# Attention outputs kept as queries x columns, their sums from a ones column in V, spilled as rows and read back transposed

## The chip, the cores and the metric

The kernel runs on one core of one Trainium2 chip. The metric is the device time of one execution in microseconds (us). TensorE (PE, with its weight loads PEld) multiplies, VectorE (DVE) and ScalarE (ACT) read its results in PSUM, GpSimd (POOL) works on SBUF alone, and SyncE (SP) issues nearly all DMAs.

## The reference

Two independent layers on 2048 tokens of width 1024; their outputs stand side by side.

```python
# A: a diagonal state-space layer (complex), P = D = 1024
Bu = einsum('bld,pd->blp', x, B_bar)
h[t] = Lam_bar * h[t-1] + Bu[t]                       # for every token
a = 2 * einsum('blp,dp->bld', h, C).real + x * Dskip
# B: attention over 64 segments of 32 tokens, 32 heads of 128, 8 memory tokens
for s in range(64):
    h = concat([mem, x[32*s:32*s+32]])                # 40 tokens
    q, k, v = h @ Wq, h @ Wk, h @ Wv                  # per head
    p = softmax(mask(q @ k.T / sqrt(128)))
    o = (p @ v) @ Wo
    mem, out_s = o[:8], o[8:]
return concat([a, b], -1)                             # bf16
```

## The kernel before

**Phase one** (`p1`, 0 to about 363 us) works on eight blocks `pc` of 128 states and, in step, on eight blocks `hb` of four heads. `stage1` forms B x for one block and 512 tokens on PE, scans it on DVE and writes the states to DRAM (`a_hs`). `v_x` computes V for four heads and 128 tokens per step; ACT copies it into `b_vst`, a tile for four steps with two buffers, and SP writes it to DRAM (`b_vx`). `load_wv` brings Wv by blocks, two buffers. `og` multiplies per-segment means of the tokens with the Wv block.

**Phase two** (`p2`, about 364 to 497 us) runs `stage2`: 32 halves, each of 16 matmuls of 512 columns (L289) from the states (`a_hl`, read back per 512 tokens) and C; DVE adds x * Dskip, which POOL has formed. Between halves the main loop puts the last two `og` (blocks 0 and 1) and the eight steps of `guess`, which multiply `ogT` with Wo (`b_wog`, 2 MB pieces, two buffers) to guess the memory tokens of all segments. The guesses become further columns of `b_xe`; `v_mem` computes their V rows.

**Attention** (`p3`, about 500 to 1071 us) goes over 16 pairs of heads `hp`, 11 units `u` each. A unit has two groups of three segments: a group is 96 tokens and 3 memory rows, 99 in all (`GW`), so a unit holds four 99 x 99 blocks (two groups, two heads). `att_front` forms four score blocks with keys on partitions and queries along the columns, takes Exp on ACT and multiplies the mask on POOL (`b_m`). `att_back`, two units later, multiplies a matrix of ones with `b_m`, so that every partition has the column sums (`psR`), takes 1/sum as Exp(-Ln) on ACT, and multiplies V (as weights) with the block: the result has head columns on partitions and queries along the columns, which is the form that the output projection needs as weights. DVE multiplies it by 1/sum into `b_ot`; SP writes `b_ot` to DRAM (`b_os`) for the first 14 pairs, the last two pairs stay in SBUF. Memory rows go to `b_omT`. The generator `proj` feeds Q and K of later pairs: 18 steps a pair, of 8 matmuls of 480 columns (L492) or 16 of 201 (L477), spread over the units, ten steps ahead.

**Output projection** (`p4`, about 1071 to 1315 us): for four blocks of 512 tokens `load_o` brings the spilled outputs (`b_ol`); each group of 32 matmuls (one per head, L607) gives 128 tokens and half of the 1024 columns. `wo0` and `wo1` are the halves of Wo, the second loaded into the space of `b_xe` when the projections are done. `check` tests the guessed memory against the computed one and sets a flag; if the guess failed, a general loop would run. It doesn't run here.

The order on each engine is made by a planner: it takes instructions in the order of the program where they are ready by its own model of time, and may draw a later instruction ahead. `keep_in_program_order` ties an instruction to its place. Tiles have a fixed number of buffers, and an instruction that needs a buffer or reused space waits for its last reader.

Of the kernel before, what the change touches and what calls it, by code (L numbers as in the profile page):

```python
# [26 lines left out]
HB = 8; HP = 16  # L27
# [8 lines left out]
NM = NTL + NMX  # L36

# [84 lines left out]
class PartA:  # L122
# [137 lines left out]
    def stage2(self, pool):  # L260
# [12 lines left out]
        for tb in range(NB):  # L273
            hl = []
            for q in range(4):
                hl.append(pool.tile([128, 2, 2, TB], BF16, name=f"a_hl{q}", bufs=2))
                (q0 if tb == 0 else k.SP).dma_start(hl[q][:], self.hs[tb][:, 2 * q:2 * q + 2, :, :])
            for tt in range(4):
                t0 = tb * TB + tt * 128
                xn = xns.pop(4 * tb + tt)  # L280
                xd = pool.tile([128, D], FP32, name="a_xd", bufs=2)
                G.tensor_tensor(xd[:], xn[:], dB[:], ALU.mult)
                ot = pool.tile([128, D], BF16, name="a_ot", bufs=2)
                for half in range(2):
                    hs = slice(half * 512, (half + 1) * 512)
                    py = k.ps("O")
                    for pc in range(PC):
                        for i in range(2):
                            PE.matmul(py[:], hl[pc // 2][:, pc % 2, i, tt * 128:(tt + 1) * 128], self.CT[:, i, pc, hs],  # L289
                                      start=(pc == 0 and i == 0), stop=(pc == PC - 1 and i == 1))  # L290
                    V.tensor_tensor(ot[:, hs], py[:], xd[:, hs], ALU.add)
                    yield
                k.SP.dma_start(self.out[0, t0:t0 + 128, 0:D], ot[:])
                if 4 * tb + tt + 3 < TT:
                    load_xn(4 * tb + tt + 3, k.SP)

class PartB:
    def __init__(self, k, x, mem0, Wq, Wk, Wv, Wo, out):  # L300
# [4 lines left out]
        self.vx = [k.drp.tile([NSLOT, 512], BF16, name=f"b_vx{i}") for i in range(HB)]  # L305
        self.vt = [k.drp.tile([NTL, 512], BF16, name=f"b_vt{i}") for i in range(HB)]
        self.os = [k.drp.tile([128, 8, T], BF16, name=f"b_os{i}") for i in range(4)]
        c = k.cst
        self.m0T = c.tile([128, KC, M], BF16, name="b_m0T")
        self.omT = c.tile([128, H, NM], BF16, name="b_omT")  # L310
# [4 lines left out]
        self.accR = c.tile([128, HP * NU], FP32, name="b_accR")  # L315
# [3 lines left out]
    def init(self, tmp):  # L319
# [11 lines left out]
        z = tmp.tile([32, 512], BF16, name="b_zero", bufs=1)  # L331
        k.V.memset(z[:], 0.0)
        for hb in range(HB):
            k.G.dma_start(self.vx[hb][64 + NMX:GX, :], z[0:GX - 64 - NMX, :])
            k.G.dma_start(self.vx[hb][T + 32:NSLOT, :], z[0:32, :])

# [37 lines left out]
    def v_x(self, hb, w):  # L374
        k = self.k
        vx = self.vx[hb]
        for q in range(4):
            st = self.wl.tile([128, 4, 512], BF16, name="b_vst", bufs=2)
            for i in range(4):
# [4 lines left out]
                k.copy("s", st[:, i, :], p[:])  # L384
# [4 lines left out]
            k.SP.dma_start(vx[s0:s0 + n * 128, :].rearrange("(i p) n -> p i n", p=128), st[:, 0:n, :])  # L389
            if q == 3:  # L390
                k.SP.dma_start(vx[0:64, :], st[0:64, 3, :])
                k.SP.dma_start(vx[T - 32:T + 32, :], st[64:128, 3, :])
# [3 lines left out]
    def og(self, hb, w, tag="R"):  # L396
        k = self.k
        p = k.ps(tag)
        for h in range(4):
            for c in range(KC):  # L400
                k.PE.matmul(p[:, h * NSEG:(h + 1) * NSEG], w[:, c, h * 128:(h + 1) * 128], self.xbar[:, c, :], start=(c == 0), stop=(c == KC - 1))
        k.V.tensor_copy(self.ogT[:, hb * 4:(hb + 1) * 4, :], p[:, 0:4 * NSEG].rearrange("p (h s) -> p h s", h=4))


    def guess(self, pool):
        k = self.k; V, PE = k.V, k.PE
        pg = k.ps("S")
        for q in range(4):
            wo = pool.tile([128, H, 256], BF16, name="b_wog", bufs=2)
            k.SP.dma_start(wo[:], self.Wo[:, :, q * 256:(q + 1) * 256])  # L410
# [21 lines left out]
    def v_mem(self, hb, w=None):  # L432
# [5 lines left out]
        st = self.wl.tile([128, 4, 512], BF16, name="b_vst", bufs=2)  # L438
        k.copy("v", st[0:NM, 0, :], p[0:NM, :])
        k.SP.dma_start(self.vx[hb][64:64 + NMX, :], st[0:NMX, 0, :])  # L440
        k.SP.dma_start(self.vt[hb][:], st[NMX:NM, 0, :])
# [58 lines left out]
    def load_v(self, hp):  # L500
        if hp < HP:
            k = self.k
            vt = self.p3a.tile([GW, NG, 256], BF16, name="b_v", bufs=2)
            hb, cs = hp // 2, slice((hp % 2) * 256, (hp % 2) * 256 + 256)
# [4 lines left out]
    def att_front(self, hp, u):  # L509
        k = self.k; PE = k.PE  # L510
# [9 lines left out]
        m = self.p3a.tile([GW, 2, 2, GW], BF16, name="b_m", bufs=4)  # L520
        mask = k.maskA if u == 0 else k.maskB
        k.G.tensor_tensor(m[:], e[:], mask[0:GW, :, :].unsqueeze(2).to_broadcast([GW, 2, 2, GW]), ALU.mult)  # L522
        return m

    def att_back(self, hp, u, m):
        k = self.k; PE, V = k.PE, k.V
        vt = self.vtile[hp]
        sm = k.ps("R")
        W4 = 4 * GW
        mf = m[:].rearrange("p a b q -> p (a b q)")  # L530
        PE.matmul(sm[:, 0:W4], k.ones[0:GW, :], mf, start=True, stop=True)
        ln = self.p3a.tile([128, W4], FP32, name="b_ln", bufs=2)
        r = self.p3a.tile([128, 2, 2, GW], FP32, name="b_r", bufs=2)
        i = hp * NU + u
        k.S.activation(ln[:], sm[:, 0:W4], ACT.Ln)  # L535
        k.S.activation(r[:].rearrange("p a b q -> p (a b q)"), ln[:], ACT.Exp, scale=-1.0, accum_out=self.accR[:, i:i + 1])  # L536
        o = k.ps("O", (128, 2, 2, GW))
        for gg in range(2):
            for hh in range(2):
                PE.matmul(o[:, gg, hh, :], vt[:, 2 * u + gg, hh * 128:(hh + 1) * 128], m[:, gg, hh, :], start=True, stop=True)  # L540
        ot = self.ot[hp]
        V.tensor_tensor(ot[:, :, 2 * u * GX:(2 * u + 2) * GX].rearrange("p h (g n) -> p g h n", n=GX),  # L542
                        o[:, :, :, 0:GX], r[:, :, :, 0:GX], ALU.mult)
        om = self.omT[:, 2 * hp:2 * hp + 2, :]
        V.tensor_tensor(om[:, :, 6 * u:6 * u + 6].rearrange("p h (g n) -> p g h n", n=3),
                        o[:, :, :, GX:GW], r[:, :, :, GX:GW], ALU.mult)
        if u == 0:
            V.tensor_tensor(om[:, :, NTL:NM], o[:, 0, :, 64:64 + NMX], r[:, 0, :, 64:64 + NMX], ALU.mult)
            if hp >= HP - 2:
                k.G.tensor_copy(ot[:, :, NSLOT:NSLOT + 64], ot[:, :, 0:64])  # L550
                k.G.tensor_copy(ot[:, :, NSLOT + 64:NSLOT + 128], ot[:, :, GX:GX + 64])
        if u == NU - 1:
            del self.vtile[hp]
            if hp < HP - 2:
                os = self.os[hp // 4]; h0 = (hp % 4) * 2
                k.SP.dma_start(os[:, h0:h0 + 2, 0:64], ot[:, :, 0:64])
                k.SP.dma_start(os[:, h0:h0 + 2, 64:T], ot[:, :, GX:T + 32])

    def att_init(self):
        self.vtile, self.ot = {}, {}  # L560
        self.load_v(0)

    def attention(self):
        units = [(hp, u) for hp in range(HP) for u in range(NU)]
        pend = []
        for n, (hp, u) in enumerate(units):
            if u == 0:
                self.load_v(hp + 1)
                self.ot[hp] = self.p3a.tile([128, 2, NSLOT + 128], BF16, name="b_ot", bufs=2)
            pend.append((hp, u, self.att_front(hp, u)))  # L570
            if len(pend) > 2:
                self.att_back(*pend.pop(0))
            yield hp, u
        for p in pend:
            self.att_back(*p)
            yield HP, 0


    def load_o(self, tb):
        k = self.k  # L580
        t = self.p4.tile([128, 28, 512], BF16, name="b_ol", bufs=2)
        for q in range(4):
            n = 8 if q < 3 else 4
            k.SP.dma_start(t[:, 8 * q:8 * q + n, :], self.os[q][:, 0:n, tb * 512:(tb + 1) * 512])
        return t

    def outproj(self, tb, ol):
# [5 lines left out]
        for tt, half in order:  # L593
# [6 lines left out]
            for h in range(H):  # L600
                if h < 28:
                    lhs = ol[:, h, tt * 128:(tt + 1) * 128]
                else:
                    ot = self.ot[h // 2]
                    s0 = NSLOT if t == 0 else t * 128 + 32
                    lhs = ot[:, h % 2, s0:s0 + 128]
                PE.matmul(p[:], lhs, self.wo[half][:, h, :], start=(h == 0), stop=(h == H - 1))  # L607
# [6 lines left out]
    def check(self):  # L614
# [3 lines left out]
        def small(name, n):  # L618
            return pool.tile([128, n], FP32, name=name, bufs=1)
        dn = small("c_dn", 4)  # L620
        V.memset(dn[:], 0.0)
        for half in range(2):
            hs = slice(half * 512, (half + 1) * 512)
            p = k.ps("P")
            for h in range(H):
                PE.matmul(p[0:NM, :], self.omT[:, h, :], self.wo[half][:, h, :], start=(h == 0), stop=(h == H - 1))
# [13 lines left out]
        for i, acc in enumerate((self.accE, self.accR)):  # L640
            a = small("c_a", HP * NU)
# [113 lines left out]
def kernel_main(tc, A_x, A_Lre, A_Lim, A_Bre, A_Bim, A_Cre, A_Cim, A_logdt, A_Dskip, B_x, B_mem0, B_Wq, B_Wk, B_Wv, B_Wo, out,  # L755
                force=False, dbg=None):
    with ExitStack() as ctx:
# [73 lines left out]
        with pool("p2", "right") as p2:  # L831
            g = b.guess(p2)
            s2 = a.stage2(p2)
            wv = [wv, b.load_wv(1)]
            for i, _ in enumerate(s2):
                if i in (2, 4):
                    b.og(i // 2 - 1, wv[i // 2 - 1], "P")
                if i > 4 and i % 2 == 1:
                    next(g, None)
                if i == 16:  # L840
# [10 lines left out]
        with pool("p3b", "right") as p3b:  # L851
# [7 lines left out]
            for n, (hp, u) in enumerate(at):  # L859
# [5 lines left out]
                while done < want:  # L865
                    next(pr)
                    done += 1
        xs.close()
# [17 lines left out]
        p3.close()  # L886
# [68 lines left out]
```

## Time and profile before

| | |
|---|---|
| Median of 8 runs | 1315.62 us (1313.8 to 1320.58) |
| Profiled execution | 1317.0 us, span 1315.2 us, mean granted clock 0.989 |
| PE busy | 1273.8 us, 97% of the span |
| DVE, ACT, POOL busy | 674.0, 427.3, 211.1 us |
| DMA | 163.15 MB, mean 124 GB/s |

All positions are microseconds from the start of the span. A row of the timeline has the start, the time from the first start to the last end of what it merges, the engine, the line, the operation with the tiles it writes and reads, and in brackets how long the engine had been idle and what released it. A matmul's recorded duration holds its latency: 512 columns show some 380 ns, but in a stream they start 216 ns apart, so that starts give the price. A transfer's bytes move after its issue.

### The profile page before, as it was taken

Reading aid. Unit: us, or ns where it says so; the run is one execution under the profiler, and the core shown is the slowest. Engines: PE = TensorE matmul, PEld = TensorE weight load, DVE = VectorE, ACT = ScalarE, POOL = GpSimd, SP = SyncE. Lnnn points to the kernel's source line nnn. Section 1 sums busy time; section 2 is a strip of 40 time slices with the busy share of each in tenths; the row PEclk is TensorE's granted clock in tenths of the full one; section 3 lists DMA queues with packets and bytes.
Section 4 is the critical chain, followed back from the end, with each engine's and each line's share of the span. In section 5 each row is a group of like instructions: output and inputs, shape, how many; then the busy total and the mean of one; then the engine's idle time right before and its main releaser. Section 6 shows DMA issues by size and latency. Waiting matters only on the chain. (4 is left out here: it accounts for less than half of the span.)

```text
span 1315.2 us, 20149 instructions
## 1 busy us (share of the span) xinstructions
PE 1273.8 (97%) x7874; PEld 659.7 (50%) x7874; DVE 674.0 (51%) x1500; ACT 427.3 (32%) x1135; POOL 211.1 (16%) x291
## 2 busy tenths in 40 slices
PE   6899899999969999999999999999999999999997
PEld 2344444444435545555555555555555544444443
DVE  6999999988821224555555555555555530001000
ACT  3333333333310001554555444545554440001000
POOL 5000000000112220222222222222222220000000
PEclk9999999999979999999999999999999989999999
DMA  9993433444389519324343434323332470403000
GB/s 229 258 212 110 120 107 108 123 129 138 115 261 309 187 48 250 83 86 121 99 133 99 133 99 133 99 85 96 87 84 83 145 237 21 136 17 127 16 23 20
DMA packets 230939, 163.15 MB, mean 124 GB/s; under 512 B 74976, under 2 KB 214864, under 8 KB 230840
## 3 DMA queue, kind: packets, MB, share of 16 engines
q1 hardware_dynamic: 229368, 158.18, 42.4%
q0 software_dynamic: 1408, 3.61, 0.9%
q8 instruction: 63, 1.03, 0.3%
q14 instruction: 36, 0.29, 0.1%
q10 hardware_dynamic: 64, 0.02, 0.0%
HBM read 95.72 MB, written 49.30 MB: 110 GB/s over the span
## 5 line engine op out<-in xcount | busy, mean ns | idle before, releaser
L383 PE MATMUL psP<-b_wv,b_xe 128*128 128x512 bf16 x1024 | 232.1, 384 | 16.4 <-DMA b_xe<-in_B_x_dram 11.6
L519 ACT ACTIVATE b_e<-psS 99x396 bf16<-99x396 f32 x176 | 88.2, 501 | 417.1 <-PE psS L516 413.9
L492 PE MATMUL psP<-b_xe,b_wq 128*128 128x480 bf16 x1024 | 222.9, 366 | 0.0
L492 PE MATMUL psP<-b_xe,b_wk 128*128 128x480 bf16 x1024 | 222.9, 366 | 0.0
L522 POOL TENSOR_TENSOR b_m<-b_e,maskB 99x396 bf16<-99x396 bf16 x160 | 139.4, 871 | 353.1 <-ACT b_e L519 353.1
L542 DVE TENSOR_TENSOR b_ot<-psO,b_r 128x384 bf16<-128x384 f32 x176 | 98.1, 558 | 189.2 <-ACT b_r L536 170.4
L383 PEld LDWEIGHTS <-b_xe 128*128 128x128 bf16 x1024 | 100.6, 99 | 141.0 <-DMA b_xe<-in_B_x_dram 13.1
L492 PEld LDWEIGHTS <-b_wk 128*128 128x128 bf16 x1024 | 97.1, 98 | 95.8
L607 PEld LDWEIGHTS <-b_ol 128*128 128x128 bf16 x896 | 87.8, 98 | 106.3 <-issue 1.7
L492 PEld LDWEIGHTS <-b_wq 128*128 128x128 bf16 x1024 | 95.7, 97 | 87.9
L64 DVE CAST b_k<-psP 128x480 bf16<-128x480 f32 (+1 forms) x192 | 97.5, 529 | 52.6 <-PE psP L492 52.0
L289 PE MATMUL psO<-t,a_hl 128*128 128x512 bf16 x512 | 113.8, 383 | 0.0
L64 DVE CAST b_q<-psP 128x480 bf16<-128x480 f32 (+1 forms) x192 | 97.3, 528 | 29.7 <-PE psP L492 29.7
L64 DVE CAST b_ost<-psP 128x512 bf16<-128x512 f32 x16 | 11.1, 692 | 193.4 <-PE psP L607 193.4
L62 ACT ACTIVATE b_vst<-psP 128x512 bf16<-128x512 f32 x128 | 74.0, 587 | 104.5 <-PE psP L383 91.6
L607 PE MATMUL psP<-t,b_ol 128*128 128x512 bf16 x448 | 100.5, 382 | 0.0
L607 PE MATMUL psP<-wo,b_ol 128*128 128x512 bf16 x448 | 99.3, 379 | 0.0
L536 ACT ACTIVATE b_r<-b_ln 128x396 f32<-128x396 f32 x176 | 94.0, 534 | 5.4
L535 ACT ACTIVATE b_ln<-psR 128x396 f32<-128x396 f32 x176 | 86.9, 494 | 0.0
L225 PEld LDWEIGHTS <-a_bt 128*128 128x128 bf16 x512 | 49.7, 98 | 62.1 <-issue 2.9
L289 PEld LDWEIGHTS <-a_hl 128*128 128x128 bf16 x512 | 49.9, 99 | 59.3 <-issue 2.2
L62 ACT ACTIVATE b_ost<-psP 128x512 bf16<-128x512 f32 x16 | 9.6, 597 | 211.2 <-PE psP L607 198.0
(197 smaller groups left out, 1297.9 us busy)
## 6 DMA issues: line engine op xcount, KB each, us to landing
b_v<-b_vx SPq DMA_DIRECT2D x16, 1056.0 KB
b_wv<-in_B_Wv_dram SPq DMA_DIRECT2D x16, 1024.0 KB
b_os<-b_ot SPq DMA_DIRECT2D x14, 992.0 KB
b_vx<-b_vst SPq DMA_DIRECT2D x24, 512.0 KB
b_ol<-b_os SPq DMA_DIRECT2D x12, 1024.0 KB
a_hs<-a_h SPq DMA_DIRECT2D x32, 256.0 KB
b_wog<-in_B_Wo_dram SPq DMA_DIRECT2D x4, 2048.0 KB
b_wq<-in_B_Wq_dram SPq DMA_DIRECT2D x16, 512.0 KB
```

What stands on the lines that cost most here:

```text
L62: self.S.activation(out, in_, ACT.Copy)
L64: self.V.tensor_copy(out, in_)
L225: PE.matmul(u[:], self.bt[:, i, c, :], self.xT[:, c, tb * TB:(tb + 1) * TB], start=(c == 0), stop=(c == KC - 1))
L289: PE.matmul(py[:], hl[pc // 2][:, pc % 2, i, tt * 128:(tt + 1) * 128], self.CT[:, i, pc, hs], start=(pc == 0 and i == 0), stop=(pc == PC - ...
L383: k.PE.matmul(p[:], self.xe[:, c, t * 128:(t + 1) * 128], w[:, c, :], start=(c == 0), stop=(c == KC - 1))
L492: PE.matmul(p[:, 0:480], w[i][:, c, hh * 128:(hh + 1) * 128], self.xe[:, c, 480 * q:480 * q + 480], start=(c == 0), stop=(c == KC - 1))
L519: k.S.activation(e[:], s[0:GW], ACT.Exp, scale=float(E) ** -0.5, accum_out=self.accE[0:GW, i:i + 1])
L522: k.G.tensor_tensor(m[:], e[:], mask[0:GW, :, :].unsqueeze(2).to_broadcast([GW, 2, 2, GW]), ALU.mult)
L535: k.S.activation(ln[:], sm[:, 0:W4], ACT.Ln)
L536: k.S.activation(r[:].rearrange("p a b q -> p (a b q)"), ln[:], ACT.Exp, scale=-1.0, accum_out=self.accR[:, i:i + 1])
L542: V.tensor_tensor(ot[:, :, 2 * u * GX:(2 * u + 2) * GX].rearrange("p h (g n) -> p g h n", n=GX), o[:, :, :, 0:GX], r[:, :, :, 0:GX], ALU.mult)
L607: PE.matmul(p[:], lhs, self.wo[half][:, h, :], start=(h == 0), stop=(h == H - 1))
```

## The change

Attention's products are turned around. The mask product of a block (99 keys x 99 queries, padded to 128 columns) becomes the weights, and V moves, with a column of ones behind each head's 128 columns (`EV` = 129). The result has queries on partitions and 128 output columns, and column 129 is the sum. So the matrix of ones, its matmul, Ln and the second Exp are gone; DVE takes a reciprocal of the sums and multiplies. Three blocks share one PSUM bank and one DVE instruction each, whatever unit they come from; at most eight blocks are kept waiting, and the PSUM buffers of the products and of the former sums are used in turn.

V's rows in DRAM have 4 x 129 elements; POOL writes the ones into `b_vst` before each spill. The outputs of all 16 pairs are collected in `b_ob` and written by five DMAs a pair to DRAM as rows of tokens (`on`) and of memory tokens (`tn`). `load_o` and `check` read them back with transposing DMAs. No output stays in SBUF for the projection; for the first block the last eight heads come in three pieces. The pool `p3` closes before the projection.

In phase two the two `og` move behind the third and fifth halves, tied to their place, their copy goes to ACT; the loads of `a_hl` and `b_wog` are tied to places in the loop; `guess` takes its steps at the even halves 10 to 24; the first Wq and Wk are loaded at half 20.

```diff
         for q in range(4):
-            st = self.wl.tile([128, 4, 512], BF16, name="b_vst", bufs=2)
+            st = self.wl.tile([128, 4, 4, EV], BF16, name="b_vst", bufs=2)
+            k.G.memset(st[:, :, :, E:EV], 1.0)
...
-                k.copy("s", st[:, i, :], p[:])
+                k.copy("s", st[:, i, :, 0:E], p[:].rearrange("p (h e) -> p h e", h=4))
...
-    def att_back(self, hp, u, m):
+    def att_back(self, blocks):
         k = self.k; PE, V = k.PE, k.V
+        hp, b0, n = blocks[0][0], blocks[0][1], len(blocks)
         vt = self.vtile[hp]
-        sm = k.ps("R")
...
-        PE.matmul(sm[:, 0:W4], k.ones[0:GW, :], mf, start=True, stop=True)
...
-        k.S.activation(ln[:], sm[:, 0:W4], ACT.Ln)
-        k.S.activation(r[:].rearrange("p a b q -> p (a b q)"), ln[:], ACT.Exp, scale=-1.0, accum_out=self.accR[:, i:i + 1])
...
-                PE.matmul(o[:, gg, hh, :], vt[:, 2 * u + gg, hh * 128:(hh + 1) * 128], m[:, gg, hh, :], start=True, stop=True)
...
+        o = k.ps(("O", "O", "R")[self.nback % 3], (128, 3, EV))
+        self.nback += 1
+        for i, (_, b, m, j) in enumerate(blocks):
+            PE.matmul(o[:, i, :], m[:, j * GW:j * GW + 128], vt[:, b // 2, (b % 2) * EV:(b % 2 + 1) * EV], start=True, stop=True)
+        r = self.accR[0:GW, hp * 2 * NG + b0:hp * 2 * NG + b0 + n]
+        V.reciprocal(r, o[0:GW, 0:n, E])
+        V.tensor_tensor(self.ob[:, b0:b0 + n, :], o[0:GW, 0:n, 0:E], r.unsqueeze(2).to_broadcast([GW, n, E]), ALU.mult)
+        if b0 + n == 2 * NG:
...
+            k.SP.dma_start(on[64:T - 64, :].rearrange("(g p) n -> p g n", p=GX)[:, :, cs], ov[0:GX, 1:NG - 1, :])
+            k.SP.dma_start(on[0:64, cs], ov[0:64, 0, :])
+            k.SP.dma_start(on[T - 64:T, cs], ov[0:64, NG - 1, :])
+            k.SP.dma_start(tn[0:NTL, :].rearrange("(g j) n -> j g n", j=3)[:, :, cs], ov[GX:GW, :, :])
+            k.SP.dma_start(tn[NTL:NM, cs], ov[64:64 + NMX, 0, :])
...
+        def back(keep):
+            while len(pend) > keep:
+                n = min(3, 2 * NG - pend[0][1])
+                self.att_back([pend.pop(0) for _ in range(n)])
...
+                pend += self.att_front(hp, u)
+                back(8)
...
     def load_o(self, tb):
...
-            k.SP.dma_start(t[:, 8 * q:8 * q + n, :], self.os[q][:, 0:n, tb * 512:(tb + 1) * 512])
+            for h0, h1 in ((0, 8),) if q < 3 or tb else ((0, 4), (4, 6), (6, 8)):
+                k.SP.dma_start_transpose(t[:, 8 * q + h0:8 * q + h1, :], self.on[q][rows, h0 * E:h1 * E])
...
+        for q in range(4):
+            k.SP.dma_start_transpose(self.omT[:, 8 * q:8 * q + 8, :], self.tn[q][:])
...
             for i, _ in enumerate(s2):
-                if i in (2, 4):
-                    b.og(i // 2 - 1, wv[i // 2 - 1], "P")
-                if i > 4 and i % 2 == 1:
-                    next(g, None)
-                if i == 16:
+                if i in (3, 5):
+                    b.og((i - 3) // 2, wv[(i - 3) // 2], "P")
+                if i in (5, 8, 12, 15):
+                    b.load_wog((5, 8, 12, 15).index(i), p2)
+                if i in (10, 12, 14, 16, 18, 20, 22, 24):
+                    next(g)
+                if i == 20:
                     b.load_wqk(0)
```

## The prediction

> **What bounds the kernel now.** I read the page's first part, then the windows by stage, then what PE waited for, then the timeline at the two places where PE is not full and in the middle of the attention stage.
>
> ```profile
> PE 1273.8 (97%) x7874; PEld 659.7 (50%) x7874; DVE 674.0 (51%) x1500; ACT 427.3 (32%) x1135; POOL 211.1 (16%) x291
> ```
> Windows (us, busy time and count of PE, PEld, DVE, ACT, POOL, granted clock, DMA share, GB/s):
> ```profile
> 355.00:370.00 15.00, 9.94 (x101) 5.48 (x99) 12.01 (x16) 4.60 (x7) 5.78 (x5) 0.89 0.62 206
> 370.00:380.00 10.00, 4.63 (x39) 2.74 (x40) 0.42 (x1) 0.00 (x0) 0.00 (x0) 0.50 1.02 274
> 560.00:1060.00 500.00, 500.00 (x3713) 292.93 (x3711) 263.44 (x672) 250.71 (x780) 136.91 (x160) 1.00 0.36 103
> 1060.00:1072.00 12.00, 8.74 (x73) 5.08 (x72) 6.47 (x21) 10.25 (x35) 5.29 (x6) 0.77 0.84 269
> 1072.00:1315.00 243.00, 235.62 (x1088) 107.39 (x1086) 14.96 (x31) 12.78 (x26) 0.00 (x0) 0.99 0.20 67
> ```
> PE is full through attention (560 to 1060) and output projection; there only fewer or shorter matmuls help. It is not full around 365 to 377 and around 1062 to 1071. The first hole, in the timeline:
> ```profile
> 364.40 1.09 PE L401 MATMUL psP<-b_xbar,b_wv 128*128 128x64 bf16 x32 [0.55 <-ACT b_vst L62]
> 375.37 1.89 PE L401 MATMUL psP<-b_xbar,b_wv 128*128 128x64 bf16 x32 [9.88 <-DMA b_wv<-in_B_Wv_dram]
> 377.07 22.57 PE L289 MATMUL psO<-t,a_hl 128*128 128x512 bf16 x96
> 356.31 1.57 POOL L277 DMA_DIRECT2D a_hl<-a_hs  x3 [33.72 <-PE psO L225]
> ```
> PE's second `og` of phase two waits 9.88 us for a weight block, with the state-space matmuls (L289) queued behind it, though their inputs were issued at 356.31 to 357.88 and the page gives 5.0 us to landing, so about 363. The second hole, at the end of attention:
> ```profile
> 1061.39 0.33 PE L531 MATMUL psR<-b_m,ones 99*128 99x396 bf16 x1
> 1070.71 0.51 PE L531 MATMUL psR<-b_m,ones 99*128 99x396 bf16 x1 [0.26 <-ACT b_ln L535]
> 1071.35 10.02 PE L607 MATMUL psP<-t,b_ol 128*128 128x512 bf16 x41
> 1081.21 1.03 PE L607 MATMUL psP<-t,b_ot 128*128 128x512 bf16 x4
> ```
> One unit of attention, PE alone:
> ```profile
> 704.94 0.34 PE L516 MATMUL psS<-b_q,b_k 128*128 128x99 bf16 x4
> 705.11 0.33 PE L531 MATMUL psR<-b_m,ones 99*128 99x396 bf16 x1
> 705.28 0.34 PE L540 MATMUL psO<-b_m,b_v 99*128 99x99 bf16 x4
> 705.47 3.40 PE L492 MATMUL psP<-b_xe,b_wk 128*128 128x480 bf16 x16
> 708.71 0.34 PE L516 MATMUL psS<-b_q,b_k 128*128 128x99 bf16 x4
> ```
> Starts, not durations, give PE's price: scores 0.17 us, sums 0.17, P times V 0.19, projection 3.24, sum 3.77. A 99-wide matmul with its weights costs 0.19 / 4 = 47 ns.
>
> The run shown took 1317.0 us for a span of 1315.2; the median of the eight is 1315.62. The sum is made against 1317.0 and then lowered by the 1.4 between.
>
> **Attention, PE.** Each of 176 units loses the ones matmul (0.17) and its four products of 99 columns (0.19) and gains four products of 129 columns with the probabilities as weights. Eight transposes of 128 columns (L427) start at 462.19 and what follows at 462.64: 56 ns each; 129 columns make 57, four 0.228. Saved: 0.36 - 0.228 = 0.132 us, times 176 = **23.2 us**, all on the bounding engine. The trace has no 129-wide product whose weights are P, so I bound it: at 47 ns (the 99-wide row) it saves 0.172 x 176 = 30.3; at 86 ns (L477, 201 wide: sixteen in 1.38 us) 2.8. I take 57, since 129 is nearest the 128-wide row.
>
> The Trainium skill ("TensorE: Matmul & The Clock Gate", section Back-to-back issue gap) speaks against this: it states some 81 ns for a sustained pair of weight load and 128-column matmul. By that four blocks cost 0.324 and the stage saves only 6.3 us, a time near 1300. The trace's 47 ns for 99-wide pairs is already far under it, and the row decides.
>
> **Attention, other engines.** ACT loses Ln and the second Exp with its accumulator read, 0.49 + 0.53 + 0.19 = 1.2 us a unit, all beside PE: nothing. DVE loses 0.56 + 0.17 a unit and gains, for each batch of three blocks, a reciprocal (0.19, L161) and a product (0.56, L542's size): 0.75 x 4/3 = 1.0. That is 0.27 x 176 = 48 us more DVE, 263 to about 311 of 500; PE's 3.65 us a unit hide it. A batch now often wants the mask product of the unit just before, where two units of delay were kept. Score start to product end was 708.71 to 710.69, 1.98 us; the shortest units (one L477 step) last 0.41 + 1.38 = 1.79 plus 0.29 until the block is wanted, 2.08. Just enough; zero, at most 0.1 x 32 = 3 us if not.
>
> The spill goes from two DMAs to five a head pair on SP (0.3 to 0.7 us each) over about 40 us; queued behind are the next weight loads, a whole pair ahead. Zero, unless SP has more than some 30 us of issue a pair.
>
> **Phase two.** `og` moves behind the third and fifth halves, its copy to ACT, idle there. The L289 matmuls can then start at about 364.0, when the last `og` of phase one is through (362.75 + 1.10), not at 377.07. Before: from 364.0 to the end of 96 of them at 399.64 is 35.6 us. After: 96 at 0.2156 (L607: 32 in 6.91 us) = 20.7, plus two `og` of 1.1 = 22.9. **Gain 12.7 us**, 9.9 of it the wait and the rest the half clock (0.50) after it. What is late next: `a_hl` at 363. If its space comes free only with DVE's last step of stage one (about 368), the matmuls start at 374 and the gain is 3. The `b_wog` loads (2 MB, 7 us at 300 GB/s) are issued five halves (17 us) ahead of use: zero; if their SP order slips, one wait of up to 7.
>
> **Phase one.** V's rows become 1032 bytes and each stage tile gets a POOL memset (0.1 to 0.2 us in like rows). DMA is saturated for the first 80 us (share 1.10 and 1.09, 235 to 241 GB/s), and some seven V writes of 0.5 MB lie in it, 2.1 us each. Unaligned rows are not in the trace: between nothing and half as long again, 7 us of DMA, of which PE would feel part (b_vst held PE for 4.7 us in all before). I take **+1.5**, ends 0 and 6. Zero fills on POOL: eight DMAs of 0.52, in a queue with nothing due: zero.
>
> **First V load.** P times V waited 1.0 us for `b_v` at 523.09. Its runs grow from 512 to 516 bytes; 1056 KB at the 265 to 314 GB/s seen from 1016 to 1020 are 3.7 us. Between nothing and double: 0 to 4. I take **+1.5**, later loads being a pair ahead.
>
> The Trainium skill ("DMA: Bandwidth & Descriptors", How a descriptor splits into AXI transactions) says that a run not starting on 256 bytes pays for the bytes before it and for the leftover. My estimate from its table is 3 to 4 transactions where an aligned 512 needs 2, which would put this term near 2 and phase one near 3; no run here has shown it.
>
> **The end of attention.** Without projection beside it the last eight sums matmuls start at 1061.39 to 1070.71, 9.3 us for seven intervals, ACT full. After: ACT 0.7, POOL 0.87, DVE 1.0 a unit, so 7.0. **Gain 2.3.** But the last two heads no longer come from SBUF. In order: DVE ends 1.7 us after output projection starts (1073.01 against 1071.27); the spill takes 1.2 to first data (1013.91 to 1015.1), 3.5 for its 960 KB, 0.6 to complete; the transposing read 1.3 to issue (L342, a quarter megabyte) and 2.6 to land (21.24 to 23.81). Together 10.9 us after projection starts, while head 30 is wanted after 30 x 0.2156 = 6.5. So 4.4 short, plus 1.2 of cold clock (41 matmuls took 10.02 against 8.84 at 1071.35), 5.6 if nothing covers. Cover exists: before, PE ran 13 matmuls of the next group before the late heads of the first. With three PSUM buffers 3 x 30 x 0.2156 = 19 us could be put there. I take **+3**, ends 0 and 6. Next is `wo1`, queued behind those reads on SP: issued 8 us in, 4 MB at 348 GB/s 12 us, there by 22; wanted at 128 x 0.2156 = 27.6. If transposes share its bandwidth it is up to 8 late.
>
> **Output projection.** The same matmuls. Its reads are now transposes: 4.2 to 4.7 us of issue each megabyte (L204, L342), 17 to 19 us for each block of 55 us of PE: hidden, until a megabyte costs 13.8. The four reads for the check: hidden if issued early, else a wait of 4.
>
> **Sum.** -23.2 -12.7 -2.3 +1.5 +1.5 +3 = -32.2; 1317.0 - 32.2 = 1284.8 for a run like the profiled one, 1283.4 by the median, said as 1283.
>
> **Rivals.**
> *A block costs more than its columns* (weights change every 129 columns): 86 ns, gain 2.8 for 23.2, time 1304. For it: PEld alone takes 98 ns a load in the records. Against: 704 loads already run 47 ns apart.
> *The hole only moves*: `a_hl` late (gain 3 for 12.7: 1293), or the read-back with `wo1` exposed (5.6 + 8 for 3: 1294). For the former: POOL's 33.72 us wait on that space. Together 1304.
> *Slower, by POOL's queue*: the memsets of ones stand in POOL's order among phase-two loads that wait for phase-one space, 31.69 us (L270) and 33.72 (L277). A memset behind one of them holds its V tile, its write, the two buffers, ACT's copies and PE. Two tiles cover 20 us each: then 12 + 14, time 1309. Fully exposed 65, time 1348. It turns the sign from 33 us exposed. Against: the order is planned by time, and the loads come later in the program.
> *The change does not do what it says*: it surely removes the ones matmuls; this has no place beyond the second rival.
>
> **How the numbers follow.** Forecast case 0.68, 1274 to 1296: about 1283, 7 less at 47 ns a block and 2 for the small terms, or 13 more with phase one, the V load, the end and the mask product at their upper ends (4.5 + 2.5 + 3 + 3). The first two rivals 0.18, 1293 to 1313. No change 0.02. POOL's queue or a mishap of that size 0.12, 1319 to 1348. The range 1275 to 1306 leaves out the slower case and the upper edge of the rivals. 0.2% is 2.6 us, about what can be told from no change: faster 0.86, same 0.02, slower 0.12.
>
> **Shown right or wrong by** the profile after: unit period 3.65 where it was 3.77 (two projection steps); no `b_wv` wait at `og`, L289 from 364; no L535 and L536; PE gap below 6 us before head 30; POOL's memsets not behind L270's wait. A unit at 3.77 or more, or PE waiting on DVE or `b_m` each unit, would make it wrong.

## Result and the profile after

The changed kernel takes 1308.41 us (median of 13 runs, 1306.63 to 1313.1); the kernel before took 1315.36 beside it. The ratio is 0.995 (95% interval 0.9941 to 0.9959), some 6.6 us where 32 were forecast. The execution shown took 1310.35 us for a span of 1308.7. Here and below a gain in us that comes from a ratio is the ratio's distance from 1 times 1316 us.

Milestones on PE say where the time went. The first two columns are the traces of before and after; the last is the kernel with three repairs that the experiments led to (e10), shown here because the losses found below are gone from it, so that the forecast's terms can be compared with it one by one.

| us from the start of the span | before | after | repaired (e10) |
|---|---|---|---|
| first state-space matmul of phase two (L289, now L297) | 377.07 | 367.71 | 362.52 |
| first Q projection (L477, now L502) | 500.63 | 498.59 | 488.02 |
| first output-projection matmul (L607, now L625) | 1071.35 | 1061.23 | 1033.54 |
| first of its second half of columns (`wo`) | 1099.99 | 1092.64 | 1061.40 |
| end of the span | 1315.2 | 1308.7 | 1277.0 |

By stage, against the prediction's terms for it:

| stage | forecast | after | repaired (e10) |
|---|---|---|---|
| to the first Q projection | -12.7 + 1.5 = -11.2 | -2.0 | -12.6 |
| to the first output-projection matmul | -23.2 - 2.3 + 1.5 = -24.0 | -8.1 | -25.2 |
| to the end | +3 | +3.6 | -0.4 |
| sum | -32.2 | -6.5 | -38.2 |

(The execution of e10 in these tables took 1279.17 us; the kernel's median is 1283.34.) The last row of the change is no hit: PE's standing before the first output-projection matmul, 12 us, lies in the row above it.

The page's first part, and the windows (columns as before: us, busy time and count of PE, PEld, DVE, ACT, POOL, granted clock, DMA share, GB/s):

```profile
PE 1257.4 (96%) x7698; PEld 650.7 (50%) x7698; DVE 715.7 (55%) x1611; ACT 250.2 (19%) x609; POOL 223.6 (17%) x340
```
```profile
355.00:370.00 15.00, 11.82 (x78) 5.38 (x77) 9.02 (x15) 4.72 (x7) 8.60 (x11) 0.88 0.70 239
370.00:380.00 10.00, 10.00 (x40) 3.95 (x39) 1.39 (x2) 0.00 (x0) 1.54 (x2) 0.83 1.12 336
...
1040.00:1060.00 20.00, 7.38 (x70) 4.41 (x68) 9.94 (x31) 3.43 (x13) 5.90 (x7) 0.73 0.47 100
1060.00:1072.00 12.00, 10.16 (x36) 3.63 (x36) 0.00 (x0) 0.00 (x0) 0.00 (x0) 0.74 1.13 253
```

PE lost its 176 sums matmuls (7698 matmuls for 7874) and is still full through attention, but 355 to 370 is still not full, and in place of a thin stretch around 1062 to 1071 there is a real hole at 1040 to 1060: 7.38 us busy of 20. What PE waited for, in all (line, tile, releaser, us, times, longest):

```profile
PE psP L625 <- DMA b_ol<-b_on: 12.7, 3, 12.0
...
PE psO L297 <- DVE a_ot L299: 3.7, 3, 2.1
...
PE psO L297 <- DMA a_hl<-a_hs: 3.2, 1, 3.2
PE psO L562 <- DMA b_v<-b_vt: 2.5, 1, 2.5
PE psO L562 <- POOL b_m L548: 1.3, 3, 0.6
```

The wait for `b_wv` (9.9) is gone, as forecast. In its place stand `b_ol` at the end of attention, `a_hl` and the writes of `a_ot` in phase two, and a longer wait for the first `b_v`.

**Attention did what was forecast, nearly.** One unit, and a double one, on PE:

```profile
616.29 0.34 PE L562 MATMUL psR<-b_v,b_m 99*128 99x129 bf16 x3
616.47 3.40 PE L517 MATMUL psP<-b_xe,b_wk 128*128 128x480 bf16 x16
...
619.88 0.52 PE L562 MATMUL psO<-b_v,b_m 99*128 99x129 bf16 x6
620.24 1.78 PE L517 MATMUL psP<-b_xe,b_wq 128*128 128x480 bf16 x8
```

Three blocks take 0.18 us from start to start, six 0.36: 60 ns each. The period of a pair follows from one block of 201 columns and the same one four pairs on, in the change (L502) and in the kernel before (L477):

```profile
567.01 1.55 PE L502 MATMUL psP<-b_xe,b_wq 128*128 128x201 bf16 x16
...
703.55 1.55 PE L502 MATMUL psP<-b_xe,b_wq 128*128 128x201 bf16 x16
```
```profile
567.55 1.55 PE L477 MATMUL psP<-b_xe,b_wq 128*128 128x201 bf16 x16
...
709.24 1.55 PE L477 MATMUL psP<-b_xe,b_wq 128*128 128x201 bf16 x16
```

A pair takes 34.14 us where it took 35.42. That is 1.29 us a pair, 20.6 for the 16.

**Phase two: POOL.** The timeline of POOL at the change of phase:

```profile
359.14 0.11 POOL L462 MEMSET b_vst<- 73x4 bf16 x1 [10.08 <-DMA b_vx<-b_vst]
...
360.24 1.61 POOL L273 DMA_DIRECT2D a_xn<-in_A_x_dram  x3
361.84 2.11 POOL L281 DMA_DIRECT2D a_hl<-a_hs  x4
```

POOL stood 10.08 us at a memset of `b_vst` from `v_mem` (L462), the ones of the memory rows of V. It needs a buffer from which phase one's last V rows are still being written out. `v_mem` itself runs 136 us later (495.14); the planner drew the memset ahead. Behind it in POOL's order stand the loads of `a_xn` and `a_hl`, which before were issued at 313.94 and, the last pieces, at 356.31. On PE, and then SP's queue:

```profile
367.71 16.90 PE L297 MATMUL psO<-t,a_hl 128*128 128x512 bf16 x64 [3.18 <-DMA a_hl<-a_hs]
...
411.26 3.61 PE L297 MATMUL psO<-t,a_hl 128*128 128x512 bf16 x16 [2.08 <-DVE a_ot L299]
```
```profile
367.53 3.19 SPq L487 DMA_DIRECT2D b_wq<-in_B_Wq_dram  x1
...
377.35 3.00 SPq L487 DMA_DIRECT2D b_wk<-in_B_Wk_dram  x1
...
382.05 2.06 SPq L281 DMA_DIRECT2D a_hl<-a_hs  x4
...
386.47 10.46 SPq L301 DMA_DIRECT2D out_dram<-a_ot  x1
```

PE waited 3.18 us for `a_hl` with `og` done, then ran 64 matmuls in 16.90 us, which at 0.2156 are 13.8: the granted clock was 0.83. On SP four loads of Wq and Wk (2 MB, 3.2 us each to issue) stand ahead of `a_xn` and the second `a_hl` although the program has them at half 20, over 70 us later (in e4 and e6 below, which keep them there, the first is issued at 438.18 and 443.82): loads around them are tied to their places, they are not. Behind them and the 2 MB of each `b_wog`, a write of an `a_ot` takes 10.46 and 7.54 us to issue, DVE (which needs that buffer) waits 26.4 us in four times, and PE 3.7 us for DVE:

```profile
DVE a_ot L299 <- DMA out_dram<-a_ot: 26.4, 4, 7.9
```

**The end of attention.** SP, then PE:

```profile
1035.43 0.48 SPq L575 DMA_DIRECT2D b_tn<-b_ob  x1
1050.29 0.32 SPq L571 DMA_DIRECT2D b_on<-b_ob  x1
...
1054.49 17.14 SPq L608 DMA_TRANSPOSE b_ol<-b_on  x6
1071.73 0.53 SPq L901 DMA_DIRECT2D wo<-in_B_Wo_dram  x1
```
```profile
1061.23 3.59 PE L625 MATMUL psP<-t,b_ol 128*128 128x512 bf16 x8 [11.96 <-DMA b_ol<-b_on]
...
1092.64 17.65 PE L625 MATMUL psP<-wo,b_ol 128*128 128x512 bf16 x81
```

SP issues nothing from 1035.9 to 1050.29. All six reads of the first block, heads 0 to 31, follow the last pair's spill: 17.14 us of issue from 1054.49. PE's last product ended near 1049, and it stood 11.96 us. In the trace of before the reads of the first heads had been issued at 1023.08:

```profile
1023.08 5.84 SPq L584 DMA_DIRECT2D b_ol<-b_os  x4
```

### The profile page after: what moved, and what is told of

Read it like the earlier page. It is cut to its first block, busy times and chain, and to the rows that moved or that the text cites. A ratio compares the mean times of both kernels' runs of the same rounds, so it can differ in the third digit from the quotient of the medians.

```text
span 1308.7 us, 19219 instructions
## 1 busy us (share of the span) xinstructions
PE 1257.4 (96%) x7698; PEld 650.7 (50%) x7698; DVE 715.7 (55%) x1611; ACT 250.2 (19%) x609; POOL 223.6 (17%) x340
## 5 line engine op out<-in xcount | busy, mean ns | idle before, releaser
L399 PE MATMUL psP<-b_wv,b_xe 128*128 128x512 bf16 x1024 | 232.4, 384 | 15.4 <-DMA b_xe<-in_B_x_dram 10.6
L625 PEld LDWEIGHTS <-b_ol 128*128 128x128 bf16 x1024 | 100.0, 98 | 136.3 <-DMA b_ol<-b_on 15.8
L625 PE MATMUL psP<-t,b_ol 128*128 128x512 bf16 x512 | 115.7, 384 | 12.9 <-DMA b_ol<-b_on 12.7
L297 PE MATMUL psO<-t,a_hl 128*128 128x512 bf16 x512 | 115.5, 385 | 6.9 <-DVE a_ot L299 3.7
L625 PE MATMUL psP<-wo,b_ol 128*128 128x512 bf16 x512 | 112.6, 379 | 0.0
L565 DVE TENSOR_TENSOR b_ob<-psO,b_accR 99x384 bf16<-99x384 f32 x160 | 85.9, 554 | 2.4
L297 PEld LDWEIGHTS <-a_hl 128*128 128x128 bf16 x512 | 49.6, 99 | 68.0 <-issue 6.3
L299 DVE TENSOR_TENSOR a_ot<-psO,a_xd 128x512 bf16<-128x512 f32 x32 | 21.9, 691 | 106.4 <-PE psO L297 80.0
L542 PEld LDWEIGHTS <-b_k 128*128 128x128 bf16 x704 | 50.1, 98 | 33.4 <-issue 1.0
L228 PE MATMUL psS<-a_xT,a_bt 128*128 128x512 bf16 x256 | 61.1, 382 | 3.4 <-DMA a_xT<-in_A_x_dram 3.4
```

The costliest lines, as they stand in the source:

```text
L228: PE.matmul(u[:], self.bt[:, i, c, :], self.xT[:, c, tb * TB:(tb + 1) * TB], start=(c == 0), stop=(c == KC - 1))
L399: k.PE.matmul(p[:], self.xe[:, c, t * 128:(t + 1) * 128], w[:, c, :], start=(c == 0), stop=(c == KC - 1))
L542: PE.matmul(s[:, gg, hh, :], kt[:, hh, g0:g0 + 128], qt[:, hh, g0:g0 + GW], start=True, stop=True)
L565: V.tensor_tensor(self.ob[:, b0:b0 + n, :], o[0:GW, 0:n, 0:E], r.unsqueeze(2).to_broadcast([GW, n, E]), ALU.mult)
L625: PE.matmul(p[:], ol[:, h, tt * 128:(tt + 1) * 128], self.wo[half][:, h, :], start=(h == 0), stop=(h == H - 1))
```

## Experiments

My theory after this comparison: the attention change is worth what was forecast, and what is missing are three losses in the order of the queues (the memset on POOL, Wq and Wk on SP, the reads behind the last spill). Rivals: the DMA engines have no room for the loads and reads whatever their order, or the change's phase-two part is not worth 12.7 us at all.

The ratios' intervals are 1 to 3 us to each side, so the difference between two of these kernels is known to some 3 us, and the sums below are to be read with that.

Each kernel has its own line numbers: output projection is L625 after, L613 in e1, L630 in e7, L632 in e10.

**e1 and e2: each part alone.** e1 is the change with the main loop, `load_h`, `load_wog` and `og` of before; e2 is the kernel before with those of the change.

```diff
 # e1, against the change; e2 makes the opposite edits in the kernel before
-                if i in (3, 5):
-                    b.og((i - 3) // 2, wv[(i - 3) // 2], "P")
-                if i in (5, 8, 12, 15):
-                    b.load_wog((5, 8, 12, 15).index(i), p2)
...
+                if i in (2, 4):
+                    b.og(i // 2 - 1, wv[i // 2 - 1], "P")
+                if i > 4 and i % 2 == 1:
+                    next(g, None)
+                if i == 16:
```

> The change without its phase-two part: the attention outputs as queries x columns, the spilled rows and the read-back stay, phase two is scheduled as before. My theory by the trace after: the phase-two part earned 2.7 us net and the attention part, with what follows it, the rest, so this kernel takes 1308.4 + 2.7 = 1311 us; PE waits 9 to 10 us for b_wv near 365 again, and about 12 us for b_ol at the start of the output projection. Rival, the phase-two part costs more later than it earns early (its loads push others back): at or below 1308. Rival, it earned more than the milestones show: 1316 or more.

> The kernel before with the phase-two part alone (og moved and its copy on ACT, loads tied to places in the order, the Wo loads spaced). If the gain was lost because POOL stood at a memset of V's ones before it could issue a_xn and a_hl, this kernel, which has no such memset, starts the stage-two matmuls near 364 instead of 367.7, and the time is 1315.4 - 2.7 - 3 to 4 = 1309 to 1310 us. If a_hl is late for another reason (its space), PE waits 3 us for it here as well and the time is 1312.7. The Wq and Wk loads are still in front of a_hl(1) and of the writes of outputs, so DVE should still wait tens of us for the writes of a_ot (about 26 us a time) in either case.

e1: 1316.04 us, ratio 0.9993 (0.9979 to 1.0006). e2: 1311.68 us, ratio 0.9969 (0.9957 to 0.9982). Alone the attention change gained nothing at all, 5 us less than I expected. What PE waited for in e1:

```profile
PE psP L613 <- DMA b_ol<-b_on: 14.3, 5, 12.5
PE psP L412 <- DMA b_wv<-in_B_Wv_dram: 13.0, 1, 13.0
```

The 20.6 us of attention are there (the same pair period), and are mostly spent: 14.3 at `b_ol`, and the wait for `b_wv` went from 9.9 to 13.0. In e2, without the memset, PE's first state-space matmuls start straight behind `og`, with no wait for `a_hl`: evidence for the memset, which e5 below moves by itself.

```profile
363.30 13.98 PE L293 MATMUL psO<-t,a_hl 128*128 128x512 bf16 x62
```

But e2's PE still loses 5.3 us behind DVE at the writes of `a_ot`, so the order on SP costs with or without the attention change.

**e4, e5, e6 and e9: the two losses of phase two.** e5 sets all the ones of `v_mem` on DVE, e6 ties Wq and Wk, e4 does both, e9 both with DVE for the first two tiles only.

```diff
-        k.G.memset(st[0:NM, 0, :, E:EV], 1.0)                          # e4, e5
+        k.V.memset(st[0:NM, 0, :, E:EV], 1.0)
-        k.G.memset(st[0:NM, 0, :, E:EV], 1.0)                          # e9, e10
+        (k.V if hb < 2 else k.G).memset(st[0:NM, 0, :, E:EV], 1.0)
-                self.k.SP.dma_start(w[:], self.Wf[i][...])             # e4, e6, e9, e10, e11
+                ld = self.k.SP.dma_start(w[:], self.Wf[i][...])
+                if hp < 2:
+                    self.k.tc.keep_in_program_order(ld)
```

> The change with two edits in phase two: the ones of V are set on DVE instead of POOL, and the first two pairs' Wq and Wk loads are tied to their place in the program, so they go behind the last load of Wo instead of ahead of the second a_hl and the writes of outputs. Theory: POOL issues a_hl by about 357 as it did before, the stage-two matmuls start near 364 (3 to 4 us), their first 44 run at the full rate (up to 3 us), and DVE's 26 us waits for the writes of a_ot go, with PE's 3.7 us behind them: 6 to 10 us in all, 1298 to 1302. Rival: a_hl waits for its space, not for POOL's memset: start stays at 367 and only the a_ot waits go, about 4 us, 1304 to 1305. Rival: the writes are slow because of the Wo loads alone and the Wq/Wk loads only come late for the attention stage: 1308 or above.

> The change with only the ones of the memory rows of V set on DVE instead of POOL. If the memset on POOL alone made a_hl late, the stage-two matmuls start at 363 to 365 as in the run with both edits, and the waits of DVE for the writes of a_ot stay (some 26 us, with 2 to 4 us of PE behind them), since the Wq and Wk loads still go first: about 1305. The run with both edits showed DVE held for 6.8 us by such a memset just before the first projections (a later tile, waiting for the write of an earlier one) and PE 3.9 us behind it; that should show here too unless the writes come at other times. If the two edits are worth nothing one by one: 1308.

> The change with only the first two pairs' Wq and Wk loads tied behind the last Wo load. If those 2 MB are what delays the second a_hl and the writes of outputs, the stage-two matmuls still start near 367 (POOL's memset is as it was), DVE's waits for the writes of a_ot fall from some 26 us to under 10, and the time falls by 2 to 4 us, to 1304 to 1306. If the Wo loads alone delay the writes, the waits stay and the time is 1308.

> The change with the Wq and Wk loads tied as in the run that did only that (1302.65, stage-two matmuls from 368.5 after a wait of 3.5 us for a_hl) and the ones of the first two memory tiles of V set on DVE, those of the later tiles on POOL as in the change. If the 4 us that the DVE memset cost before the first projections came from a later tile's memset standing in DVE's queue, that wait (DVE at b_vst, PE at b_q) is gone, a_hl is in time (start near 364), and the time is 1302.65 - 3 to 5 = 1298 to 1300. If DVE still stands at a memset: 1302 to 1304.

| | us | ratio (95%) | first L297 | PE waits: `a_hl`, `a_ot`, `b_q` |
|---|---|---|---|---|
| after | 1308.41 | 0.995 (0.9941 to 0.9959) | 367.71 | 3.2, 3.7, none |
| e5 memset on DVE | 1308.06 | 0.9954 (0.9938 to 0.9971) | 362.46 | none, 7.7, 4.3 |
| e6 loads tied | 1302.65 | 0.9901 (0.9884 to 0.9917) | 368.47 | 3.7, none, none |
| e4 both | 1304.61 | 0.9918 (0.9904 to 0.9932) | 364.54 | none, 1.7, 3.9 |
| e9 both, two tiles | 1297.45 | 0.9855 (0.984 to 0.987) | 363.44 | none, 2.1, none |

The tied loads are worth 6.4 us (0.995 to 0.9901), more than I expected; DVE's 26 us at the writes of `a_ot` are gone. The memset moved to DVE in e5 brings the start forward as e2 said, and gains nothing: DVE now stands at such a memset itself, at a later tile, whose buffer is being written out, with the copies of the first projections behind it. DVE in e5, and PE behind it:

```profile
506.68 0.06 DVE L462 MEMSET b_vst<- 73x4 bf16 x1 [6.89 <-DMA b_vt<-b_vst]
```
```profile
508.27 4.84 PE L517 MATMUL psP<-b_xe,b_wq 128*128 128x480 bf16 x16 [4.32 <-DVE b_q L67]
```

That is why e4 is no better than e6. e9 leaves the later tiles on POOL, which has nothing due there, and the wait for `b_q` is gone: together 12.5 us (0.995 to 0.9855), of which the memset is 6.1. In e6, e9 and e10 the wait for the first `b_v` is gone too, with V's runs as long as in the change.

**e3, e7 and e8: the end of attention.** When the last projection step is out, the space of `b_xe` and of Wq and Wk is free. e3 closes it there and issues, tied, the four reads of heads 0 to 27 and Wo's second half; e7 leaves Wo to the place behind the reads of the last heads; e8 has e3's early reads and gives the last pair's spills, the late reads and Wo to ACT to issue.

```diff
+                if done == 18 * HP and not b.early:
+                    b.early = True
+                    xs.close()
...
+                    ol = b.load_o(0, p4a, 1)                                               # heads 0 to 27
+                    tc.keep_in_program_order(k.SP.dma_start(wo1, b.Wo[:, :, 512:D]))       # e3 only
...
+            b.load_o(0, part=2, t=ol)                                                      # heads 28 to 31
             tc.keep_in_program_order(k.SP.dma_start(wo1, b.Wo[:, :, 512:D]))               # stays here in e7, e10
...
+            Q = k.S if hp == HP - 1 else k.SP                                              # e8: spills by Q,
+                ld = (k.S if part == 2 else k.SP).dma_start_transpose(t[...], self.on[q][...])
```

> The change with one thing moved: the projections' space is closed when the last projection step is emitted, and the four transposing reads of heads 0 to 27 for the first row block and the load of the second half of Wo are issued there, ahead of the spills of the last head pair; only the last four heads are read after them. Theory: the 11 us lost at the end of attention are the reads standing in SP's order behind the last spill; then the first output-projection matmul starts within 1 us of the last attention matmul, and the time falls by 8 to 11 us, to 1298 to 1300. Rival: the round trip of the last heads (spill, then transposing read, some 11 us) is the bound whatever the order; output projection then starts early but stops before head 28, and the gain is 0 to 4 us. Rival: DMA bandwidth near 1050 (share 1.04) is the bound: early reads delay the spills and the gain is under 3 us.

> The run with early reads, but the 4 MB of Wo behind the reads of the last four heads instead of ahead of the last spills. In that run the last spills were issued only from 1052.1 to 1066.7 (8.6 and 5.5 us of issue where 0.3 to 2 are usual) and PE stood 5.6 us before the last heads. If the Wo load held them, the spills now take under 4 us of issue, PE stands under 2 us, and the time is 1300.7 - 4 to 6 = 1295 to 1297. If the four transposing reads ahead of them hold them (their data take as long to move), the spills are still late, and Wo comes later as well: 1300 or more.

> The run with early reads, with the last pair's spills, the reads of the last four heads and then the 4 MB of Wo issued by ACT, which has nothing else to do then, instead of SP. If SP's queue held the last spills, they go out within 3 us of the last product (1050.4), the reads land by 1063, and PE, which has 84 matmuls (18 us) before it needs them, does not stand: 1295 to 1296. If the time is lost in the DMA engines themselves (the transposing reads ahead occupy all of them), PE still stands 4 to 6 us: 1300 to 1301.

e3: 1300.74 us, ratio 0.988 (0.9863 to 0.9897), 9 us better than the change. e7: 1294.52 us, ratio 0.9832 (0.9811 to 0.9853), 15.5 us better. e8: 1301.94 us, ratio 0.9884 (0.986 to 0.9908). SP in e3, then in e7, and e7's PE:

```profile
1051.45 0.53 SPq L905 DMA_DIRECT2D wo<-in_B_Wo_dram  x1
1052.08 8.60 SPq L571 DMA_DIRECT2D b_on<-b_ob  x1
1060.77 5.47 SPq L573 DMA_DIRECT2D b_on<-b_ob  x1
```
```profile
1034.99 14.93 SPq L611 DMA_TRANSPOSE b_ol<-b_on  x4
1050.01 0.53 SPq L571 DMA_DIRECT2D b_on<-b_ob  x1
1050.64 2.60 SPq L573 DMA_DIRECT2D b_on<-b_ob  x1
...
1058.25 0.54 SPq L912 DMA_DIRECT2D wo<-in_B_Wo_dram  x1
```
```profile
1049.01 27.93 PE L630 MATMUL psP<-t,b_ol 128*128 128x512 bf16 x125
1076.78 23.47 PE L630 MATMUL psP<-wo,b_ol 128*128 128x512 bf16 x108
```

With Wo ahead of them the same two spills take 8.60 and 5.47 us to issue; behind them Wo is still in time. In e7 PE goes from the last product into output projection without a wait, 27.93 us for the 125 matmuls on record. The round trip of the last heads, from the last product near 1049 to their reads issued at 1058, lies under heads 0 to 27 of three groups, 84 matmuls; e3 too ran about as many (82 on record, 1048.12 to 1066.66) before it had to wait, 4.0 us. Space was not what held the reads in the change: e3's tile lies in the same freed space, behind `wo1`, and its reads are issued at 1035.71. So the order of SP is the cause, and the DMA engines had room for all of it. e8 doesn't settle what it was for: PE stood 5.47 us until 1061.71, before ACT issued the last read at 1063.56, so it waited for another piece, and its matmuls were in another order than in e3. Why is open; e7 made it needless.

**e10: all repairs (the edits of e7 and e9); e11: e2 with the edit of e6**, which is the same without the attention change.

> All three repairs of the change: early reads with Wo behind them (1294.5 alone), Wq and Wk tied (6 us alone) and the memsets of the first two memory tiles on DVE (3 to 5 us). If the three losses lie in different places and add, the time is 1294.5 - 6 - 4 = 1284, with PE's waits for b_ol, a_hl, a_ot and b_v all under 1 us; my sum before the run was 1283.4 with all of these at nothing or nearly so. If a repair only moves a wait (the tied loads now arriving at the first projection, the reads in the way of the last weight loads), it stays at 1288 or above.

> The kernel before with the phase-two part and the Wq and Wk loads tied: everything of the run with all repairs except the attention change (and its read-back at the end). It says what the attention change is worth when nothing else holds PE. The phase-two part alone gave 1311.7 with 5.3 us of PE waiting for the writes of a_ot; tied loads should take most of that away: 1305 to 1307. Then the attention change itself is worth 1283.3 - 1306 = 22 to 23 us, near the 23.2 + 2.3 - 3 of the prediction. If a good part of what the repairs gave came from the attention change's own cost in phase two, this kernel is at 1300 or below and the attention change is worth 17 or less.

e10: 1283.34 us (1279.17 to 1286.47), ratio 0.9754 (0.9739 to 0.977). e11: 1304.14 us, ratio 0.9904 (0.9886 to 0.9921). e10 beats both kernels. What its PE waited for (the first four rows), and its two places:

```profile
PE psP L399 <- DMA b_xe<-in_B_x_dram: 12.3, 4, 8.2
PE psP L399 <- ACT b_vst L65: 4.7, 6, 2.9
PE psS L228 <- DMA a_xT<-in_A_x_dram: 3.5, 2, 2.0
PE psO L297 <- DVE a_ot L299: 1.6, 1, 1.6
```
```profile
362.52 7.07 PE L297 MATMUL psO<-t,a_hl 128*128 128x512 bf16 x31
```
```profile
1034.42 27.14 PE L632 MATMUL psP<-t,b_ol 128*128 128x512 bf16 x123
```

The three rows above `a_ot` are phase one's, which the kernel before has as well. The losses lay in different places and nearly add: 15.5 (e7) and 12.5 (e9) are 28, e10 is 25.8 better than the change. e11 puts the phase-two part at 12.6 us once its loads are in order, and e10 against e11 the attention change at 19.7 (0.9904 to 0.9754), read-back included; I had expected 22 to 23.

## Why the prediction was wrong, step by step

- **Phase two, gain 12.7: mechanism and size right, not realised in the change.** e11 measures 12.6 us. Two steps failed. The start "at about 364.0" took the issue of `a_hl` at 356.31 from the trace of before, and I put the small POOL instructions down as a queue "with nothing due": I counted the memsets of phase one and the zero fills, but not that of `v_mem`, which can be drawn ahead to where its tile's last writer is still being written out. And the step on the `b_wog` loads ("issued five halves ahead of use: zero; if their SP order slips, one wait of up to 7") never listed Wq and Wk, which the diff moves from half 16 to 20 in the text and which went the other way in SP's order. After: 6.4 us for the loads, 6.1 for the memset.
- **The end of attention, +3 taken (0 to 6): the largest miss.** The chain of 10.9 us for the last two heads was nearly right (8.3 of it up to the end of the issue, for 9.1 in e7, from 1049.01 to 1058.15), and so was its cover: e7 hides it completely. The step that failed is the silent one, that heads 0 to 27 would be there as they were before, so that their matmuls cover it. Their reads stood behind the last spill on SP; 17.14 us of issue that I had put under output projection ("4.2 to 4.7 us of issue each megabyte: hidden") were in front of it. It cost 15.5 us against e7. The bound of 6 was the bound of the wrong piece.
- **Attention on PE, gain 23.2: 20.6.** A block costs 60 ns, not 57; 47 and 86 ns were its bounds. The 81 ns that the Trainium skill states ("TensorE: Matmul & The Clock Gate", Back-to-back issue gap) is not what this stream shows, and the 6.3 us by it would have been wrong by 14. The tail's gain, 2.3, was 3.5: from the last score beside a projection to the last product 6.6 us for 10.1.
- **The mask product, DVE and ACT: zero, as taken.** PE waited 1.3 us in all for `b_m`, and what DVE does more in attention (busy 298.5 us from 500 to 1071 before, 345.7 from 498 to 1061 after) lies beside PE.
- **First V load, +1.5: right in the change (2.5 for 1.0), for the wrong reason.** With the loads tied the wait is gone with the same 516-byte runs, so it was the queue. My estimate of near 2 from the Trainium skill ("DMA: Bandwidth & Descriptors", How a descriptor splits into AXI transactions) happens to lie beside the number; no run here shows a cost of those runs.
- **Phase one, +1.5: about +0.5.** The last `og` of phase one starts at 362.4 to 363.2 in the three kernels with rows of 512 elements, and at 363.3 on average in the ten with 516 (361.5 to 365.4): a difference inside the scatter.
- **Rivals.** "The hole only moves" came, in both its places, and its 1304 was near 1308.4: I had priced a late `a_hl` with 9.7 (3 gained for 12.7) and the read-back with 10.6 more than the 3 taken. The runs put the two places at 12.5 and 15.5. The mechanisms were others, though: not the space of `a_hl` but POOL's order and SP's, and not `wo1` behind the reads but the first reads behind the last spill, so that the near number is luck. "POOL's queue" had the parts exchanged: I looked for a memset behind a load, and it was the loads behind a memset, worth 6 us and not the 26 to 65 that I had priced. Its argument against ("the order is planned by time, and the loads come later in the program") was the error, since a planned order may draw a later memset ahead.
- **Small readings.** The 1.2 us to a spill's first data (1013.91 to 1015.1) were read from a load of V, the DMA issued at 1013.91; and for `wo1` 8 us plus 12 make 20 and not 22. Neither changes the +3, which was chosen between bounds.

That e10 lies at 1283.34 and the forecast at 1283 says that the sum had the price of the change's work nearly right; it left out the order in which that work is issued. That the two agree so closely is partly luck: attention on PE gave 2.6 us less than its term and the tail 1.2 more, and the +3 of the end and the +1.5 of the first V load are not paid in e10. The execution of e10 in the tables is better than the sum by 1.4, 1.2 and 3.4 us by stage; it lies 4.2 us below its kernel's median and the one of before 1.6 above its own, which makes most of these 6 us. What lets e10 vary from 1279.17 to 1286.47 is open.

## To carry to other kernels

Ask of each small instruction that a change adds, and of each load that it does not tie, what it would hold if it were drawn to the front of its queue: the price of a memset is that of the loads behind it. Where a result no longer stays on chip, list the issue order of every read that the next stage starts with, not only the latest one; the early pieces are the cover. And when a large gain shows up small, undo it by halves: one part alone gained nothing and the other 4 us, yet 20 and 12.6 were in them.

## What the runs showed of the hardware

How long SP takes to issue the same DMA varied with what stood ahead of it: a 512 KB load of Wq took 3.19 us at 367.53 and 0.43 us in e4 at 438.18; a write of 256 KB to `out_dram` 10.46 us at 386.47 and 0.34 at 411.83; the last pair's 960 KB spill 8.60 us with 4 MB of Wo issued just ahead of it (e3) and 0.53 us without (e7). That the time is a backlog being worked off is my reading of these numbers. Rows of V of 1032 bytes for 1024, read in runs of 516 for 512, cost no time that these runs could tell from nothing. Transposing reads of 3.5 MB took 14.93 us to issue (e7), 4.3 us a megabyte.
